# V of token tiles 8 to 15 by a seven-product identity on pairs of tiles, in a fused attention and feed-forward kernel

## The chip, the cores and the metric

The kernel runs on one core of a Trainium2 chip. The metric is the device time of one execution in microseconds (us). The engines of the core work side by side, each through its own queue in order: TensorE (PE: matrix products into the PSUM banks), VectorE (DVE), ScalarE (ACT), GpSimd (POOL, which here only adds and subtracts in SBUF), and SyncE (SP, which issues most of the DMAs).

## The reference

```python
xn = _layernorm(x)                                   # x: 1 x 2048 x 1024, bf16
qkv = xn @ wqkv                                      # wqkv: 1024 x 3072; 32 heads of 32
phi = lambda t: jnp.where(t > 0, t + 1, jnp.exp(t)) + 1e-6
pq, pk = phi(q), phi(k)
kv = einsum("bhsd,bhse->bhde", pk, v);  z = einsum("bhsd->bhd", pk)
o  = (pq @ kv) / (pq @ z + 1e-6)
s  = o @ wo
g  = silu((silu(xn @ w_gate) * (xn @ w_up)) @ w_down)   # 3584 hidden features
return x + s * g
```

The linear attention needs K and V of all 2048 tokens before the first output can be formed. Tokens are cut into 16 tiles of 128.

## The kernel before, in words

The order of the work on PE, DVE, ACT and POOL is written out by hand: each engine takes its instructions in the order in which the program emits them (`manual_schedule`). The work has these stages:

- K and V. For each token tile `i` the loop over `c` runs four products (`emit_Bmm`, L541 to L549): `c` 0 and 1 are the halves of K, 2 and 3 the halves of V. Each is eight matmuls of 128x128 by 128x512 into one of three PSUM banks (`psB`). `emit_Bev` (L551) evacuates a bank: V by an ACT copy, K by `phi`: ACT makes exp (L154) and, up to tile 8, relu (L161) into SBUF; DVE adds a constant (L162) and combines the two (L163). From tile 9 on DVE works in place on the bank (L157, L163). `emit_C(i)` (L564) then adds tile `i`'s K transposed times V to the sum `kvz`, which stays in PSUM.
- In between, DVE prepares the later tiles: `ln_pre` (statistics, L475, L476; the reciprocal root on POOL, L497 and L498) and `emit_N` (normalises, L503; a DMA then transposes the tile into `xnT`).
- `so_stat` (ACT squares rows of W_v and W_o with a sum, L623), `so_pow2` (sums them over partitions on PE and makes a power of two on DVE, L626 to L638), `wo_scale` (DVE scales W_o by it, L641).
- `prep_step` (L352) prepares one tile of the feed-forward weights, in a pipeline of steps: a DMA load on SP, the store of the one before last on SP, an ACT square with a sum (L288), a one-column matmul (L292), three tiny DVE instructions for a power of two (L297 to L301) and a DVE scaling (L311), and four POOL sums (L323 to L326). A weight is squared three steps after its load, scaled and summed in the step after that, and stored one step later still; 22 weights take 26 steps. Four steps lie in tiles 4 to 7, twelve in tiles 8 to 15, two among the Q products of block 0, four each in blocks 1 and 2.
- Q and attention. Tokens go in four blocks of 512. `emit_Q` (L178) makes one of the eight feature tiles of Q, of a block, in five banks (`ps2`); `phi` there takes three ACT instructions and one DVE one (L148 to L151) or the form of K. `emit_ND` (L721) forms the quotient for one token tile: eight small products in one bank group that has no second copy, then DVE (L739, L743, L747). It needs all eight Q feature tiles of its block. Block 0's four run between the Q products of block 1.
- POOL forms sixteen slices of sums of W_o (`To`, L780); the output projection of blocks 2 and 3 uses the seven-product identity with them, and the feed-forward part uses the same identity throughout.

Of the kernel before, what the change touches and what calls it, by code (L numbers as in the profile page):

```python
# [21 lines left out]
def kernel(  # L22
# [37 lines left out]
    NPE = 4  # L60
    NWARM = 11
    NPREP = 13
    NWE = 7
    LEAD = 6
    NPK = 8
    SO_ST = [(i, c) for i in (2, 3, 4, 5) for c in (0, 2)] + [(i, c) for i in (6, 7, 8, 9) for c in (0, 2)]
    PREP_AT = ((4, 1), (5, 1), (6, 1), (7, 1))
    SO_PW = [(7, 1), (10, 1)]
    RXN = 32
# [74 lines left out]

    def emit_phi(work, t_ps, dst, W, in_place=False, act=False):
        e_t = work.tile([P, W], FP32, name="e_t", tag="e_t")
        if act:
            nc.scalar.activation(out=e_t[:], in_=t_ps, func=ACT.Relu, scale=-1.0)  # L148
            nc.scalar.activation(out=e_t[:], in_=e_t[:], func=ACT.Exp, scale=-1.0)
            nc.scalar.activation(out=t_ps, in_=t_ps, func=ACT.Relu)  # L150
            phi_late.append(lambda: nc.vector.scalar_tensor_tensor(out=dst, in0=e_t[:], scalar=EPS, in1=t_ps,  # L151
                                                                   op0=ALU.add, op1=ALU.add))
            return
        nc.scalar.activation(out=e_t[:], in_=t_ps, func=ACT.Exp)  # L154
        if in_place:
            r = t_ps
            nc.vector.tensor_scalar(out=r, in0=t_ps, scalar1=0.0, scalar2=EPS, op0=ALU.max, op1=ALU.add)  # L157
        else:
            r_t = work.tile([P, W], FP32, name="r_t", tag="r_t")
            r = r_t[:]  # L160
            nc.scalar.activation(out=r, in_=t_ps, func=ACT.Relu)  # L161
            nc.vector.tensor_scalar(out=r, in0=r, scalar1=EPS, scalar2=None, op0=ALU.add)  # L162
        nc.vector.scalar_tensor_tensor(out=dst, in0=e_t[:], scalar=1.0, in1=r,  # L163
                                       op0=ALU.min, op1=ALU.add)
# [126 lines left out]
    def emit_st1(key, ps):  # L291
        nc.tensor.matmul(ps, lhsT=ones[:], rhs=st_tiles.pop(key)[:], start=True, stop=True, skip_group_check=True)  # L292
        st_tiles[key] = ps
# [55 lines left out]

    stat_ps = [None]  # L350

    def prep_step(between=None):  # L352
# [36 lines left out]

    kvz_ps = psa_tile("kvz")[1]  # L390
    with ExitStack() as p1:
# [149 lines left out]
        def emit_Bmm(i, c):  # L541
            tok = slice(i * P, (i + 1) * P)
            kv_ps = psB.tile([P, CW], FP32, name="kv_ps", tag="B")
            kv_banks[(i, c)] = kv_ps
            for dc in range(DC):
                mm = nc.tensor.matmul(kv_ps[:], lhsT=xn_ap(dc, tok), rhs=wkv_sb[:, dc, c * CW:(c + 1) * CW],  # L546
                                      start=(dc == 0), stop=(dc == DC - 1))
                if dc == 0 and c == 0:
                    marks[("B", i)] = mm  # L549

        def emit_Bev(i, c):  # L551
            kv_ps = kv_banks.pop((i, c))
            if i not in pkv_tiles:
                pk_sb = work.tile([P, D], BF16, name="pk_sb", tag="pk_sb")
                pkv_tiles[i] = (pk_sb, v_bufs[i % 2])
            pk_sb, v_sb = pkv_tiles[i]
            if c < NCC:
                emit_phi(phiw, kv_ps[:], pk_sb[:, c * CW:(c + 1) * CW], CW, in_place=i >= 9)
            else:
                vc = c - NCC  # L560
                nc.scalar.copy(out=v_sb[:, vc * GPC:(vc + 1) * GPC, 0:P],
                               in_=kv_ps[:].rearrange("p (g c) -> p g c", c=P))

# [13 lines left out]

        warm = work.tile([P, CW], BF16, name="warm", tag="warm")
        nc.vector.memset(warm[:], 0.0)
        wps = psB.tile([P, CW], FP32, name="warm_ps", tag="B")  # L580
        for k in range(NWARM):
            nc.tensor.matmul(wps[:], lhsT=warm[:, 0:P], rhs=warm[:], start=True, stop=True)
        stat_ps[0] = lambda: psC.tile([P, 1], FP32, name="st_ps", tag="C")[:]
# [36 lines left out]
        def so_stat(q):  # L620
            src = wkv_sb[:, q, D:2 * D] if q < 8 else wo_sb[:, q - 8, :]
            with nc.allow_low_precision("a bound that only sets a power of two"):
                nc.scalar.activation(out=pqT_of(0)[:, 2 * (q % 4):2 * (q % 4) + 2, :].rearrange("p a b -> p (a b)"),  # L623
                                     in_=src, func=ACT.Square, accum_out=so_st[:, q:q + 1])

        def so_pow2(h):  # L626
            ps = stat_ps[0]()
            for q in range(8 * h, 8 * h + 8):
                nc.tensor.matmul(ps, lhsT=ones[:], rhs=so_st[:, q:q + 1], start=q == 8 * h, stop=q == 8 * h + 7,
                                 skip_group_check=True)  # L630
# [12 lines left out]

        for i in range(2, NT):
            for c in range(NCH):
                if (i, c) in SO_ST:
                    q = SO_ST.index((i, c))
                    so_stat(q)
                if (i, c) in SO_PW:
                    so_pow2(SO_PW.index((i, c)))  # L650
                if c == 3 and i in WO_SC:
                    wo_scale(WO_SC.index(i))
                if (i, c) != (2, 0):
                    emit_Bmm(i, c)
                if c == 0:
                    emit_C(i - 1)
                emit_Bev(i, c)
                if (i, c) == (2, 2):
                    emit_TR(3)
                if c % 2 == 1:  # L660
                    for k in N_AT.get(2 * i + c // 2, ()):
                        emit_N(k)
                        if 0 <= k - NPE < NCC:
                            load_qo(wo_sb, wo_v, k - NPE)
                    for k in PRE_AT.get(i, ())[c // 2:c // 2 + 1]:
                        ln_pre(k)
                if (i, c) in PREP_AT:
                    prep(1)
                if i >= 8 and c % 2 == 1:
                    k = 2 * (i - 8) + c // 2  # L670
                    prep(12 * (k + 1) // 16 - 12 * k // 16)
        ps1.close()
# [12 lines left out]
        for g in range(1, G):  # L685
            emit_Q(0, g, act=g in (3,5,7))
            if g in (2, 5):
                prep(1)
            phi_flush()
# [24 lines left out]
    with ExitStack() as p2:  # L714
# [10 lines left out]
        def emit_ND(b, t, nd):  # L725
# [12 lines left out]
            for j0, j1, ng in ((0, NJ - 1, GPT), (NJ - 1, NJ, G - (NJ - 1) * GPT)):  # L738
                nc.vector.tensor_scalar(  # L739
                    out=rden[:, j0 * GPT:(j1 - 1) * GPT + ng, :].rearrange("p (j g) h -> p j g h", j=j1 - j0),  # L740
                    in0=nd[:, j0:j1, 0:ng, P:P + HPG], scalar1=EPS,
                    scalar2=rc_all[:, CWO + 1:CWO + 2], op0=ALU.add, op1=ALU.mult)
            nc.vector.reciprocal(out=rden[:, 0:G, :], in_=rden[:, 0:G, :])  # L743
# [116 lines left out]
        def nd_item(b, t):  # L860
            def f():
                raw, nd = psa_tile("nd")

                def nd_ot():
                    emit_ND(b, t, nd)
                    emit_OT(b, t)
                if 0 < b < NB - 1:
                    stat_ps[0] = lambda: raw[:, 0, 511:512]
# [1062 lines left out]
```

## Time and profile before

| what | us |
|---|---|
| median of 3 runs (lowest to highest) | 751.65 (750.5 to 752.22) |
| the profiled execution, its span | 751.34, 749.6 |
| PE busy in the span | 741.9 |
| DVE, ACT, POOL busy in the span | 590.6, 385.6, 403.2 |
| in 25 to 70 (tiles 2 to 7): PE, DVE, ACT, POOL busy of 45 | 45.0, 33.27, 34.77, 6.16 |
| in 85 to 115 (tiles 10 to 13): PE, DVE, ACT, POOL busy of 30 | 30.0, 25.08, 20.80, 29.52 |
| in 145.5 to 159.5 (block 0's quotients, block 1's Q): PE, DVE, ACT, POOL busy of 14 | 14.0, 12.04, 12.43, 13.92 |

PE is busy in nearly every slice of the span. The granted TensorE clock is 1.0 throughout. A busy PE says that a matmul was under way. Other engines may be idle without cost as long as PE never waits for them.

### The profile page before, as it was taken

The numbers are of one execution on the slowest core, as the hardware profiler recorded it, in microseconds if no ns is written. First come the engines' busy times: TensorE is split into PE (matmuls) and PEld (weight loads), VectorE is DVE, ScalarE is ACT, GpSimd is POOL, SyncE is SP. The second block draws the span as 40 slices with busy tenths as digits, with TensorE's granted clock in tenths as the row PEclk, the third lists the DMA queues.
The fourth block names the chain that finished last, engine by engine and source line by source line (L and its number), as shares of the span: only waits on it lengthen the run. The fifth ranks groups of instructions, "written<-read, shape, count | busy, mean of one in ns | idle before, by whom it ended". The sixth has DMA issues, their size and how long they took to land.

```text
span 749.6 us, 11280 instructions
## 1 busy us (share of the span) xinstructions
PE 741.9 (99%) x3962; PEld 370.8 (49%) x3962; DVE 590.6 (79%) x1046; ACT 385.6 (51%) x556; POOL 403.2 (54%) x435
## 2 busy tenths in 40 slices
PE   8999999999999999999999999999999999999997
PEld 3544444454454444444444444644444444467665
DVE  6577788887697688788889886587877767688897
ACT  5677866889965666667557511232222232322023
POOL 0111799998640255858586027310766676770076
PEclk9999999999999999999999999999999999999999
DMA  9957799869678668787889417998698889668854
GB/s 316 337 139 149 219 329 307 310 151 263 208 202 273 229 223 289 274 322 279 320 270 417 169 48 295 269 373 282 225 306 305 307 290 347 244 221 315 279 172 92
DMA packets 132425, 194.21 MB, mean 259 GB/s; under 512 B 36384, under 2 KB 106144, under 8 KB 122640
## 3 DMA queue, kind: packets, MB, share of 16 engines
q1 hardware_dynamic: 123600, 158.69, 65.3%
q0 software_dynamic: 7328, 32.31, 11.6%
q10 hardware_dynamic: 1440, 2.49, 1.0%
q8 instruction: 31, 0.51, 0.3%
q14 instruction: 26, 0.21, 0.1%
HBM read 122.68 MB, written 63.96 MB: 249 GB/s over the span
## 4 chain that ended last, share of the span: by engine, by line
PE 94%; DVE 3%; DMA 1%; ACT 1%; issue 1%; POOL 1%; DVEq 0%; ACTq 0%; POOLq 0%; SPq 0%
PE zw L958 25%; PE kv_ps L546 15%; PE xb L958 13%; PE q_ps L183 6%; PE dzw L1252 6%; PE yb L958 6%; PE dm L1533 5%; PE dm L1497 3%; PE fx L808 3%; PE s_ps L766 3%; PE dx L1252 2%; PE dy L1252 2%; PE dm L1252 1%; PE kvz L568 1%; PE nd L735 1%
## 5 line engine op out<-in xcount | busy, mean ns | idle before, releaser
L958 PEld LDWEIGHTS <-w_sb 128*128 128x128 f16 (+1 forms) x1568 | 152.0, 98 | 183.1 <-issue 0.5
L958 PE MATMUL xb<-xnT,w_sb 128*128 128x512 bf16 x448 | 115.0, 379 | 0.0
L546 PE MATMUL kv_ps<-wkv_sb,xnT 128*128 128x512 bf16 x512 | 113.8, 379 | 0.6 <-ACT xnT L535 0.4
L958 PE MATMUL zw<-xnT,w_sb 128*128 128x512 bf16 x448 | 105.9, 379 | 0.0
L958 PE MATMUL zw<-S,w_sb 128*128 128x512 f16 x448 | 105.8, 379 | 0.0
L323 POOL TENSOR_TENSOR w_sb<-w_sb 128x512 f16<-128x512 bf16 x42 | 50.7, 1206 | 99.9 <-DVE w_sb L311 51.2
L288 ACT ACTIVATE w_sb<-w_sb 128x2048 bf16<-128x2048 bf16 x42 | 79.9, 1902 | 3.5 <-DMA w_sb<-in_B_w_up_dram 2.4
L546 PEld LDWEIGHTS <-xnT 128*128 128x128 bf16 x512 | 48.3, 97 | 56.0 <-ACT xnT L535 0.8
L1139 POOL TENSOR_TENSOR w_sb<-w_sb 128x512 f16<-128x512 f16 (+3 forms) x48 | 50.0, 1063 | 28.5 <-DMA w_sb<-wd 27.5
L1034 ACT ACTIVATE sg<-cg 128x1024 bf16<-128x1024 f32 x28 | 29.6, 1057 | 57.6 <-DVE cg L1027 57.6
L183 PE MATMUL q_ps<-xnT,wq_sb 128*128 128x512 bf16 x256 | 58.4, 379 | 0.4 <-DVE pqT L151 0.4
L958 PE MATMUL yb<-S,w_sb 128*128 128x512 f16 x224 | 57.5, 379 | 0.0
L1027 DVE SCALAR_TENSOR_TENSOR cg<-zw,rc_all,s 128x1024 f32<-128x1024 f32 x28 | 35.9, 1283 | 25.3 <-PE zw L958 12.8
L986 DVE SCALAR_TENSOR_TENSOR s<-yb,rc_all,s 128x512 f32<-128x512 f32 x42 | 31.4, 749 | 27.9 <-ACT s L985 27.9
L324 POOL TENSOR_TENSOR w_sb<-w_sb 128x512 f16<-128x512 bf16 x42 | 50.7, 1207 | 3.3
L1230 POOL DMA_DIRECT2D out_dram<-io x16 | 8.7, 544 | 80.7 <-DVE io L1229 80.5
L326 POOL TENSOR_TENSOR w_sb<-w_sb 128x512 f16<-128x512 bf16 x42 | 50.3, 1197 | 0.0
L325 POOL TENSOR_TENSOR w_sb<-w_sb 128x512 f16<-128x512 bf16 x42 | 49.8, 1185 | 0.0
L985 ACT ACTIVATE s<-xb,rcl 128x512 f32<-128x512 f32 x14 | 9.6, 687 | 65.0 <-PE xb L958 65.0
L985 ACT ACTIVATE s<-xb,rc_all 128x512 f32<-128x512 f32 x42 | 28.4, 675 | 21.9 <-issue 12.7
L311 DVE TENSOR_SCALAR w_sb<-w_sb,cs_all 128x2048 bf16<-128x2048 bf16 x35 | 36.2, 1035 | 3.5 <-DVE cs_all L301 0.8
L183 PEld LDWEIGHTS <-wq_sb 128*128 128x128 bf16 x256 | 24.4, 97 | 28.1 <-issue 0.6
(232 smaller groups left out, 1364.4 us busy)
## 6 DMA issues: line engine op xcount, KB each, us to landing
w_sb<-pk_g SPq DMA_DIRECT2D x27, 1024.0 KB, 6.4
pk_g<-w_sb SPq DMA_DIRECT2D x14, 1024.0 KB, 5.0
w_sb<-pk_u SPq DMA_DIRECT2D x14, 1024.0 KB, 8.5
pk_u<-w_sb POOLq DMA_DIRECT2D x13, 1024.0 KB, 5.5
w_sb<-l SPq DMA_DIRECT2D x12, 896.0 KB, 5.6
l<-w_sb POOLq DMA_DIRECT2D x9, 896.0 KB, 7.7
w_sb<-in_B_w_gate_dram SPq DMA_DIRECT2D x14, 512.0 KB, 6.6
w_sb<-in_B_w_down_dram SPq DMA_DIRECT2D x28, 256.0 KB, 4.7
```

The costliest lines, as they stand in the source:

```text
L183: nc.tensor.matmul(q_ps[:], lhsT=wq_sb[:, dc, g * P:(g + 1) * P], rhs=xn_ap(dc, btok), start=(dc == 0), stop=(dc == DC - 1))
L288: nc.scalar.activation(out=junk, in_=raw_view(key, t), func=ACT.Square, accum_out=asum[:])
L323: nc.gpsimd.tensor_tensor(out=T1, in0=b12, in1=b11, op=ALU.subtract)
L324: nc.gpsimd.tensor_tensor(out=T2, in0=b22, in1=T1, op=ALU.subtract)
L325: nc.gpsimd.tensor_tensor(out=T3, in0=b22, in1=b12, op=ALU.subtract)
L326: nc.gpsimd.tensor_tensor(out=T4, in0=b21, in1=T2, op=ALU.subtract)
L546: mm = nc.tensor.matmul(kv_ps[:], lhsT=xn_ap(dc, tok), rhs=wkv_sb[:, dc, c * CW:(c + 1) * CW], start=(dc == 0), stop=(dc == DC - 1))
L958: mm = nc.tensor.matmul(out, lhsT=lhs(k), rhs=rhs(k), start=(first and k == 0), stop=(k == HK - 1), skip_group_check=True)
L985: nc.scalar.activation(out=s1[:], in_=x_[:], func=ACT.Copy, scale=rc)
L1139: nc.gpsimd.tensor_tensor(out=b(o_), in0=b(a_), in1=b(b_), op=ALU.subtract)
L1252: nc.tensor.matmul(out, lhsT=lhs, rhs=rhs, start=first, stop=lastk, skip_group_check=True)
L1533: nc.tensor.matmul(out, lhsT=lhs, rhs=w[:, j], start=i == 1 and j == 0, stop=j == NQ - 1, skip_group_check=True)
```

## The change

For V of token tiles 8 to 15, two token tiles (rows) and the two halves of the 1024 inputs make a 2x2 block matrix, and W_v is cut in 2x2 blocks likewise. The eight block products of the pair become seven of four matmuls each, with sums of inputs (`S1` to `S4`) and of weights (`T1` to `T4`). The parts:

- `so_pow2(0)` runs at tile 5 and not 7, so the squares of W_v are made earlier (`SO_ST`); DVE then copies the four quarters of W_v, scaled, into the still unused Q feature tiles of blocks 0 and 1 (`wv_copies`, four instructions of 128x2048); POOL forms the four weight sums in place there, each in four slices of 128x512 (`wv_sum`, at (5,0), (5,2), (6,0), (7,2)).
- Tile 7 makes V first, then K; after its V, DVE scales three quarters of W_v in place (`wv_scale`), and after `emit_C(7)` it scales the sum so far (`kv_scale`).
- Each pair makes its products in three banks `X`, `W`, `Y` of `psB`, with the K products in between in the two banks of `psC`. ACT copies X to Y, keeps two partial results in SBUF as float32 over an unused quarter of W_v (`kept_v`), and writes the finished halves; DVE adds the two others (`v_add`).
- `S1` and `S2` are made by DVE, `S3` and `S4` by POOL (`emit_xsum`), before each pair. K is evacuated in place from tile 7 on.
- Preparation steps in tiles 8 to 15 fall from twelve to eight; block 0's Q products take three and not two, and block 0's quotients 1 to 3 one each. The sums of squares there use spare columns of the last `kvz` bank.

The quotient no longer multiplies by W_v's scale (L740). The core of the diff:

```diff
-    SO_PW = [(7, 1), (10, 1)]
+    SO_PW = [(5, 0), (10, 1)]
...
-                emit_phi(phiw, kv_ps[:], pk_sb[:, c * CW:(c + 1) * CW], CW, in_place=i >= 9)
+                emit_phi(phiw, kv_ps[:], pkv_of(i)[0][:, c * CW:(c + 1) * CW], CW, in_place=i >= NV - 1, between=between)
...
+        def wv_copies():
+            for dst, q in ((T1b, (0, 0)), (T3b, (0, 1)), (T2b, (1, 1)), (T4b, (1, 0))):
+                nc.vector.tensor_scalar(out=dst, in0=wv_q(*q), scalar1=c_v, scalar2=None, op0=ALU.mult)
+        def wv_sum(n):
+            T1, T2, T3, T4 = Tv
+            o_, a_, b_ = ((T1, T3b, T1b), (T3, T2b, T3b), (T2, T2b, T1), (T4, T4b, T2))[n]
+            for k in range(HG):
+                nc.gpsimd.tensor_tensor(out=o_[:, k], in0=a_[:, k], in1=b_[:, k], op=ALU.subtract)
+        WV_SUM = ((5, 0), (5, 2), (6, 0), (7, 2))
...
+        def emit_xsum(i):
...
+            nc.vector.tensor_tensor(out=S1, in0=a21, in1=a22, op=ALU.add)
+            nc.vector.tensor_tensor(out=S2, in0=S1, in1=a11, op=ALU.subtract)
+            nc.gpsimd.tensor_tensor(out=S3, in0=a11, in1=a21, op=ALU.subtract)
+            nc.gpsimd.tensor_tensor(out=S4, in0=a12, in1=S2, op=ALU.subtract)
...
+            if i >= NV and n == 1:
+                prep(1)
+        for i in range(2, NV):
+            for n, c in enumerate(range(NCH) if i < NV - 1 else (2, 3, 0, 1)):
+                before(i, n)
                 if (i, c) != (2, 0):
                     emit_Bmm(i, c)
+                if (i, n) == (NV - 1, 2):
+                    wv_scale()
+                if n == 0:
                     emit_C(i - 1)
                 emit_Bev(i, c)
...
+                behind(i, n)
+                if (i, n) == (NV - 2, 3):
+                    emit_xsum(NV)
...
+        for i in range(NV, NT, 2):
+            j = i + 1
...
+            mm4(X, xn_q(i, 0), wv_q(0, 0), True)
+            nc.scalar.copy(out=Y[:], in_=X[:])
+            mm4(W, S1, Tv[0], True)
+            emit_Bmm(i, 0)
+            if i == NV:
+                emit_C(i - 1)
+            emit_Bev(i, 0)
...
+            mm4(Y, S2, Tv[1], False)
+            mm4(X, xn_q(i, 1), wv_q(1, 0), False)
+            if i == NV:
+                kv_scale()
+            nc.scalar.copy(out=kept_v(0), in_=by_half(W[:]))
+            nc.scalar.copy(out=v_half(i, 0), in_=by_group(X))
+            nc.scalar.copy(out=kept_v(1), in_=by_half(Y[:]))
+            behind(i, 1)
+            before(i, 2)
+            emit_Bmm(i, 1)
+            if i > NV:
+                emit_C(i - 1)
+            mm4(Y, S3, Tv[2], False)
+            emit_Bev(i, 1, between=lambda: v_add(j, Y, 0))
...
+            emit_Bmm(j, 0)
+            emit_Bev(j, 0)
...
+            mm4(Y, xn_q(j, 1), Tv[3], False)
+            mm4(W, S4, wv_q(1, 1), False)
+            nc.scalar.copy(out=v_half(j, 0), in_=by_group(Y))
+            v_add(i, W, 1)
+            if j + 1 < NT:
+                emit_xsum(j + 1)
+            behind(j, 1)
+            before(j, 2)
+            emit_Bmm(j, 1)
+            emit_C(i)
+            emit_Bev(j, 1)
...
-            if g in (2, 5):
+            if g in (2, 4, 6):
                 prep(1)
...
-                if 0 < b < NB - 1:
+                if b < NB - 1 and (b, t) != (0, 0):
                     stat_ps[0] = lambda: raw[:, 0, 511:512]
                     prep_step(nd_ot)
```

## The prediction

> **What bounds the kernel now.** I read the page first, for the share of each engine; then the chain that ended last, for the places where PE itself waits; then the order of time on DVE, ACT and POOL around the change. The page (columns: slices of the span; groups by line):
>
> ```profile
> span 749.6 us, 11280 instructions
> PE 741.9 (99%) x3962; PEld 370.8 (49%) x3962; DVE 590.6 (79%) x1046; ACT 385.6 (51%) x556; POOL 403.2 (54%) x435
> ...
> L546 PE MATMUL kv_ps<-wkv_sb,xnT 128*128 128x512 bf16 x512 | 113.8, 379 | 0.6 <-ACT xnT L535 0.4
> ```
>
> PE sets the time; V and K cost 113.8 us and wait 0.6. In the chain (start, length, what), products follow each other from tile 2 to the end of block 0 without a gap. The first break is in block 1, where a DVE scaling of a weight takes 4.23 us:
>
> ```profile
> 40.64 6.91 PE kv_ps L546 x32
> 47.55 0.46 PE kvz L568 x8
> ...
> 145.37 0.47 PE nd L735 x8
> ...
> 164.43 4.23 DVE w_sb L311
> ```
>
> So 32 matmuls take 6.91 us, 0.216 each, and work removed from PE is worth its full time only while no other engine is late. How near they are shows in the order of time (start, length, engine, line). DVE and POOL around 97 us:
>
> ```profile
> 96.73 1.15 POOL L325 TENSOR_TENSOR w_sb<-w_sb 128x512 f16<-128x512 bf16 x1
> 97.84 1.60 POOL L326 TENSOR_TENSOR w_sb<-w_sb 128x512 f16<-128x512 bf16 x1
> ...
> 97.09 1.34 DVE L311 TENSOR_SCALAR w_sb<-w_sb,cs_all 128x2048 bf16<-128x2048 bf16 x1
> 98.35 1.64 DVE L641 TENSOR_SCALAR wo_sb<-wo_sb,cs_all 128x2048 bf16<-128x2048 bf16 x1
> ```
>
> A scaling from SBUF to SBUF (0.74 at its shortest) and a POOL sum (1.15) do not overlap: each waits for the other and they take turns. Then around block 0's quotients:
>
> ```profile
> 144.29 0.69 DVE L151 SCALAR_TENSOR_TENSOR pqT<-e_t,q_ps 128x512 bf16<-128x512 f32 x1 [0.22 <-ACT q_ps L150]
> ...
> 145.00 0.66 PEld L735 LDWEIGHTS <-pqT 128*128 128x128 bf16 x8
> ...
> 163.61 4.50 POOL L780 TENSOR_TENSOR To_sb<-wo_sb,To_sb 128x512 f16<-128x512 bf16 x4
> ...
> 164.43 4.23 DVE L311 TENSOR_SCALAR w_sb<-w_sb,cs_all 128x2048 bf16<-128x2048 bf16 x1
> ```
>
> The first quotient's weights load 0.02 us after DVE finishes the last Q feature tile: no slack there. And against four sums of the `To` form in a row, the scaling got no turn until the row was over.
>
> The sum goes against the profiled execution's own 751.34 us (span 749.6, 1.7 around it), 0.3 under the median 751.65 of three runs. No change means within 0.2%, 1.5 us.
>
> **A. Products.** Each pair does 28 matmuls for V where it did 32: 16 fewer, at 0.216, is -3.45. Float16 ones show the same 379 ns as bf16 ones (L958), so nothing is lost on the type.
>
> **B. Tiles 5 to 8.** DVE is 33.27 busy of 45 us in tiles 2 to 7, and gets there: a power of two (0.75, as at 64.63 to 65.3), four copies (0.75 each, L311's shortest), `S1` and `S2` (0.42 to 0.66 in L801 to L804, 1.0 together), three scalings of W_v (2.25), and tile 7 in place (0.70 and 0.69 for each half, 2.9 against 2.4). PE's own clock: tile 5 starts at 45.82, plus 0.18 for the eight small matmuls; with 1.73 a product and 0.46 a `kvz` step it wants `C(5)` at 55.1, `X` at 68.1, and `W` at 69.0. `W` takes the bank of K(7,0), so it needs DVE through that evacuation. DVE is free at 48.05 (end of the L476 at 47.80). Until then it must do: 0.75 + 3.0 + tile 5's K 2.4 + two normalisations and two statistics 4.0 + tile 6's K 2.4 + the same 4.0 + sums 1.0 + one normalisation and statistics 2.0 + scalings 2.25 + K(7,0) 1.45 = 23.25, hence 71.3. That is 2.3 late even if POOL never interferes: the low end.
>
> POOL now puts sixteen slices of 1.11 us in the same stretch, where it had 1 us a tile. Queued on POOL behind them are the roots (L497, L498) for tiles 10 to 15, which the normalisations need; I find those in time. For scalings and normalisations I take turns, as at 97 us. For K's last step from SBUF (L163, two float32 inputs) no row lies next to POOL work: beside it, with one input in PSUM, it keeps 0.69; the two-input L1228 goes from 0.42 to 0.91. I let L163 pass freely and `S1`, `S2` wait. Then `T1`'s slices start at 50.4; the fourth copy ends at 52.8, K(5) at 56.1 (PE waits 1.0); `T3`'s and `T2`'s slices push tile 6's work to 67.8, the sums to 70.2, the first scaling to 73.5 (`X` wanted at 69.1: 4.3), K(7,0) to 77.0 (`W` wanted at 74.4: 2.6). B = 7.9. If L163 waits too, the same walk gives 2.7 + 1.7 + 4.1 + 3.0 = 11.5: the high end with turns. The cover for pricing the earlier squares (ACT) and the six XnT transposes on SP at nothing is idle time: ACT 34.77 of 45, SP waits on nothing new here; if it went, 1.25 a square.
>
> **C. The pairs.** PE alone needs 60 matmuls and two `kvz` steps, 13.9 a pair. DVE: 5.8 for K, 1.4 for two adds (0.69, L1255), 1.0 sums, 3.3 for two preparations, plus normalisations and `kv_scale` (about 1.4 each) in the first, `wo_scale` (2.6) in the next two: 14.3, 14.7, 14.1, 10.6. ACT is in order: behind `X`'s second product come two copies (0.5 each), the preparation's square (1.9), in the first pair a square of W_o (1.25), and only then K's exp; DVE's first step and `v_add` (0.7 each) follow, and `Y`'s last product waits on that add. From the end of `X` that is 0.5 + 0.5 + 1.9 + 0.6 + 1.4 = 4.95 with gaps 5.05, against 1.73 + 0.46 + 0.86 + 1.73 = 4.8 on PE: 0.25 late; in the first pair (no `kvz` step there) 6.3 against 4.3: 2.0. In pairs 10 and 12 `wo_scale` goes ahead of the second add, and `C(i)` is 0.75 late. C = 2.0 + 3 x 0.25 + 2 x 0.75 = 4.2; between 0 (ACT's square slips behind) and 6 (the POOL turns again). Four preparations fewer free 7.6 of ACT and 18 of POOL there, but PE did not wait on those before.
>
> **D. Block 0.** A preparation moved here brings all its instructions: load and store on SP, square 1.9 on ACT, one small matmul, 0.55 + 0.75 or more on DVE, 4.6 on POOL. The Q products of block 0 get one more: ACT ends the last feature tile 18.3 after the first Q product starts, not 16.7, and the first quotient, with no slack (above), goes 1.3 late. Block 0's quotients get three. ACT works 1.77 on each Q tile of block 1, two make 3.54 where PE takes 3.93, and two squares of 1.9 now lie ahead of the last: its feature tile is ready at 37.2, and block 1's first quotient wanted it at 34.8: 2.4 late. Sum 3.7; low end 2. Queue order: the added preparations' POOL sums fall behind the sixteen `To` slices (18 us), and SP's store of each waits for them with the next load and the quotient's transpose behind it; by the same walk the loads are late by up to 3.4 us in block 1, where eight S and Q items are run ahead, so I price it at 0 with 3.4 as the upper bound.
>
> Sum: 751.34 - 3.45 + 7.9 + 4.2 + 3.7 = 763.7. The rest of the change (quotient's constant, spare columns for small sums) is free: no instruction more.
>
> **Rivals.**
> *The lateness is swallowed.* PE's run-ahead over three K and five Q banks takes up DVE's and ACT's lag, as it did in 10 to 159 us at 84% busy DVE. Place: `W`'s bank. It decides if DVE reaches K(7,0)'s end by 69.0, in 21 us for my 23.25, and ACT likewise saves its 2 us in block 0. Then only A and about 1 remain: 749. Against it: the counted rows, and the 0.02 us.
> *DVE never waits for POOL* (POOL yields always): B 2.3, C 2.5, D 3.7: 756.4. The alternating rows speak against it.
> *All two-input steps wait too:* B 11.5: 767.3. L1228's rows speak for it. By the Trainium skill ("SBUF — State Buffer", Who interferes with whom) a VectorE instruction with two SBUF inputs contends with a GpSimd one that reads SBUF, and whichever comes second is blocked until the first finishes, which is this rival; the turns at 97 us agree with its blocking, the 4.23 us, over three further ends of a sum, do not.
> *DVE gets no turn in a row of slices.* The 4.23 us against L780 is the only row in which a scaling meets this very form, and `wv_sum` and block 0's three scalings would meet it. In tiles 5 to 8, rows of four and eight slices hold DVE until K(7,0) ends near 83: B 14. In block 0, a scaling asked for at 26.8 after its first Q product waits for the end of `To` near 41; the next quotient waits with it: 14 more. 751.34 - 3.45 + 14 + 4.2 + 17.7 = 784. For T sums of the same shape at 183 us DVE did get its turn (0.82).
>
> **How the numbers follow.** Chances: swallowed 0.18; DVE never waits 0.22; my walk 0.25; two-input steps wait 0.15; no turns 0.20, half of it under 780 where only one of the two places shows it. The forecast is 763.7, itself between 759 and 768. Range 748.5 to 780: below lies 0.06, above 0.12. Faster 0.18; same, from the low edge of the second case, 0.04; slower 0.78.
>
> **What would show it.** Right: PE idle before `C(5)`, before the first pair's `X` and `W` (released by DVE) and before block 1's first quotient; DVE copies, L162 and L503 longer than 0.75, 0.43 and 0.52 while `wv_sum` runs. Wrong: no PE idle time from 50 to 80; a first quotient of block 1 that follows its Q product at once; or a scaling in block 0 of 4 us and more (the last rival).

## The result and the profile after

The changed kernel takes 786.5 us (median of four runs, 785.4 to 787.9), the kernel before 751.4 in the same session: 1.0468 times as long, with a 95% interval of 1.0446 to 1.049. The forecast was 763.7, its range ended at 780. The sign was right, the size was not: 35 us were lost where 12 were expected, and they were lost in other places.

The profiled execution took 787.9 (span 786.1), 1.4 above its median, and is set against the 751.3 (span 749.6) of before. First the page, its span and engines.

```profile
span 786.1 us, 11254 instructions
PE 743.1 (95%) x3883; PEld 370.5 (47%) x3946; DVE 607.5 (77%) x1071; ACT 385.0 (49%) x556; POOL 433.4 (55%) x459
```

PE is as busy as before (743.1 against 741.9) although 16 products are gone, and it stands for 43 us where it stood for 8. (This trace has 3883 product records for 3946 weight loads: 63 products are under way but not recorded.) So nothing was bought, and the question is where PE stands. The waits of PE by what ended them (total, times, longest) answer it:

```profile
PE nd L295 <- DVE tot L301: 9.5, 1, 9.5
PE nd L295 <- ACT w_sb L291: 4.3, 4, 1.8
PE vx L757 <- DVE wkv_sb L682: 3.8, 1, 3.8
PE kvz L582 <- DVE tot L301: 3.2, 3, 1.7
PE kvz L582 <- DVE pk_sb L166: 3.1, 2, 1.6
PE vw L757 <- DVE pk_sb L166: 2.3, 1, 2.3
PE kvz L295 <- DVE kvz L686: 1.5, 1, 1.5
...
PE kv_ps L554 <- ACT wkv_sb L791: 1.0, 2, 0.5
PE kv_ps L554 <- DMA wkv_sb<-in_A_wqkv_dram: 0.7, 1, 0.7
```

The lines with `vx`, `vw` and `pk_sb` are the first pair and tiles 5 and 6 (9.2 us together, forecast as B). The lines where `kvz` waits for `tot` or for L686, and K's product for L791, lie in the pairs (6.0). The `nd` lines lie in the blocks, and the first of them, 9.5 us in one piece, was not in the forecast at all. The last line is a wait near 9 us, at the start of this one execution.

Three points of the trace divide the span into stages: the end of the last `kvz` product, the first product of block 0's quotients (`nd`), and the first product into `xb` in the feed-forward part. Their times, and the stages between them, for most of the runs (us):

| run | last `kvz` product ends | from the first `nd` to the first `xb` product | median time |
|---|---|---|---|
| before | 129.8 | 99.9 | 751.4 |
| after | 146.5 | 118.1 | 786.5 |
| before, preparations moved | 129.5 | 118.5 | 769.1 |
| the same, S store on SP | 129.8 | 107.4 | 759.5 |
| the same as the third, `To` spread | 129.4 | 113.0 | 763.7 |
| before, S store on SP alone | 129.7 | 99.7 | 751.1 |
| before, `To` spread alone | 129.4 | 106.1 | 757.8 |
| after, `To` spread | 145.7 | 109.8 | 777.6 |
| after, S store on SP | 146.4 | 107.5 | 776.2 |
| after, no W_v sums | 136.1 | 119.8 | 778.8 |
| after, preparation one stage later | 142.2 | 119.2 | 783.2 |
| after, in place from tile 5 | 143.2 | 118.1 | 782.8 |
| after, 28 idle products added | 143.9 | 116.5 | 781.8 |

Between the first two points lie 15.4 us in both kernels. Of the 36.5 us between the two profiled executions, 16.8 arise up to the last `kvz` product and 18.2 in the blocks; the last 1.5 arise in the feed-forward part of this one execution (506.0 us, against 504.1 to 505.7 in the other profiles) and belong to no step. Nor do 0.9 of the 16.8: in this execution alone a product waits 0.65 us for the load of its weights near 9 us, and the first `kvz` step starts at 25.1 us, where it starts between 23.9 and 24.4 in all other runs. That leaves 15.9.

Up to the last `kvz` product the 15.9 divide as follows. The removed products give -3.45 (16 at 0.216). The gaps of tiles 5 to 8 give 9.2, those of the pairs 6.0. Behind the gaps of `X` and `W` products run at half pace, 2.1 more. And each stop costs 0.16 beyond its gap, since the last product ahead of it isn't overlapped by a next one (0.379 to its end against 0.216 to the next start): the 11 stops in these gaps are 1.8. The sum is 15.65; some 0.2 stay open.

Here is PE from tile 5 to the first pair, in order of time (start, length, engine, line, what; in brackets the idle time ahead and what ended it):

```profile
57.91 0.40 PE L582 MATMUL kvz<-v_sb,pk_sb 128*128 128x129 bf16 x4 [1.62 <-DVE pk_sb L166]
...
66.92 0.40 PE L582 MATMUL kvz<-v_sb,pk_sb 128*128 128x129 bf16 x4 [1.46 <-DVE pk_sb L166]
...
76.26 1.55 PE L757 MATMUL vx<-wkv_sb,xnT 128*128 128x512 bf16 x4 [3.76 <-DVE wkv_sb L682]
80.16 1.89 PE L757 MATMUL vw<-pqT,xs 128*128 128x512 f16 x4 [2.34 <-DVE pk_sb L166]
...
84.82 1.02 PE L757 MATMUL vy<-pqT,xs 128*128 128x512 f16 x4
```

`C(5)`, `X` and `W` wait for DVE where the forecast had put them (1.0, 4.3 and 2.6 there), and `C(6)` waits too. The four products of `W` take 1.89 us, the four of `Y`, of the same kind, 1.02. DVE in the same stretch:

```profile
54.30 1.52 DVE L166 SCALAR_TENSOR_TENSOR pk_sb<-e_t,r_t 128x512 bf16<-128x512 f32 x1
...
57.16 0.69 DVE L166 SCALAR_TENSOR_TENSOR pk_sb<-e_t,r_t 128x512 bf16<-128x512 f32 x1
...
78.08 0.69 DVE L166 SCALAR_TENSOR_TENSOR pk_sb<-e_t,kv_ps 128x512 bf16<-128x512 f32 x1
```

K's last step with both inputs in SBUF (L166, `e_t` and `r_t`) takes 1.52 while a row of four W_v slices runs on POOL (50.83 to 56.84), and 0.69 just behind that row. With one input in PSUM (`kv_ps`, tile 7) it takes 0.69 beside three slices too (POOL has them from 77.31 to 80.67). So steps with two SBUF inputs wait for GpSimd as well, which was one of the rivals.

Now the blocks. POOL, SP and ACT around the long stand of block 1, one fence for each (on the queues of SP and ACT the lines are DMA issues):

```profile
183.09 4.49 POOL L930 TENSOR_TENSOR To_sb<-wo_sb,To_sb 128x512 f16<-128x512 bf16 x4
...
191.44 1.16 POOL L330 TENSOR_TENSOR w_sb<-w_sb 128x512 f16<-128x512 bf16 x1
```

```profile
192.63 0.33 SPq L345 DMA_DIRECT2D pk_g<-w_sb  x1
...
197.63 0.33 SPq L345 DMA_DIRECT2D pk_g<-w_sb  x1
```

```profile
192.47 0.66 ACT L919 ACTIVATE s_sb<-s_ps,s_sc 128x512 bf16<-128x512 f32 x1
203.94 0.34 ACTq L922 DMA_DIRECT2D s_dram<-s_sb  x1
204.38 0.60 ACT L149 ACTIVATE e_t<-q_ps 128x512 f32<-128x512 f32 x1 [11.25 <-DMA pk_g<-w_sb]
```

A preparation's sums (L327 to L330) stand on POOL behind the sixteen sums of `To`, which end at 187.6. SP's store of that preparation (L345) is issued at 192.63, and SP has issued nothing since 174.4 (the end of its issues of L228). The next store leaves at 197.63. ACT has finished an S tile at 193.1 and is to issue the store of it (L922); in the trace it is released only when SP's second store has landed (at 203.86), although the two have no data in common. Both stores raise the same semaphore in the trace's records (number 107), and the later one in the program waits on it before it is issued. Behind the store in ACT's order stand the exponentials of Q, and so PE stands for 9.5 us.

### The profile page after: what moved, and what is told of

Read it like the earlier page. It is cut to its first block, busy times and chain, and to the rows that moved or that the text cites. A ratio compares the mean times of both kernels' runs of the same rounds, so it can differ in the third digit from the quotient of the medians.

```text
span 786.1 us, 11254 instructions
## 1 busy us (share of the span) xinstructions
PE 743.1 (95%) x3883; PEld 370.5 (47%) x3946; DVE 607.5 (77%) x1071; ACT 385.0 (49%) x556; POOL 433.4 (55%) x459
## 5 line engine op out<-in xcount | busy, mean ns | idle before, releaser
L1108 PE MATMUL xb<-xnT,w_sb 128*128 128x512 bf16 x421 | 113.2, 379 | 2.5 <-ACT sg L1183 1.0
L327 POOL TENSOR_TENSOR w_sb<-w_sb 128x512 f16<-128x512 bf16 x42 | 49.8, 1185 | 113.6 <-DVE w_sb L315 50.9
L1108 PE MATMUL zw<-xnT,w_sb 128*128 128x512 bf16 (+1 forms) x447 | 105.8, 379 | 0.1
L554 PE MATMUL kv_ps<-wkv_sb,xnT 128*128 128x512 bf16 x373 | 88.1, 381 | 2.8 <-ACT wkv_sb L791 1.0
L554 PEld LDWEIGHTS <-xnT 128*128 128x128 bf16 x384 | 36.6, 98 | 48.3 <-issue 7.0
L1177 DVE SCALAR_TENSOR_TENSOR cg<-zw,rc_all,s 128x1024 f32<-128x1024 f32 x28 | 35.9, 1283 | 24.4 <-PE zw L1108 13.3
L328 POOL TENSOR_TENSOR w_sb<-w_sb 128x512 f16<-128x512 bf16 x42 | 49.5, 1177 | 3.3
L330 POOL TENSOR_TENSOR w_sb<-w_sb 128x512 f16<-128x512 bf16 x42 | 50.5, 1202 | 0.0
L329 POOL TENSOR_TENSOR w_sb<-w_sb 128x512 f16<-128x512 bf16 x42 | 49.4, 1175 | 0.0
L152 DVE SCALAR_TENSOR_TENSOR pqT<-e_t,q_ps 128x512 bf16<-128x512 f32 x27 | 18.2, 682 | 31.4 <-ACT q_ps L151 31.3
L186 PEld LDWEIGHTS <-wq_sb 128*128 128x128 bf16 x256 | 24.4, 98 | 27.6 <-issue 0.5
```

Of the source, the lines that this page charges most:

```text
L186: nc.tensor.matmul(q_ps[:], lhsT=wq_sb[:, dc, g * P:(g + 1) * P], rhs=xn_ap(dc, btok), start=(dc == 0), stop=(dc == DC - 1))
L327: nc.gpsimd.tensor_tensor(out=T1, in0=b12, in1=b11, op=ALU.subtract)
L328: nc.gpsimd.tensor_tensor(out=T2, in0=b22, in1=T1, op=ALU.subtract)
L329: nc.gpsimd.tensor_tensor(out=T3, in0=b22, in1=b12, op=ALU.subtract)
L330: nc.gpsimd.tensor_tensor(out=T4, in0=b21, in1=T2, op=ALU.subtract)
L1108: mm = nc.tensor.matmul(out, lhsT=lhs(k), rhs=rhs(k), start=(first and k == 0), stop=(k == HK - 1), skip_group_check=True)
```

## The experiments

The reading above makes two claims about the blocks: the `To` sums make SP late, and ACT's store carries that lateness to PE. The rival is that ACT and the loads are simply overloaded, or late from the pairs. For tiles 5 to 8 the claims are turns between DVE and POOL on top of 2.3 us of DVE's own work; for the pairs, the place of the small sums; for the slow products, the stand ahead of them.

**The S store on SP's queue.**

```
-                nc.scalar.dma_start(out=s_dram[r0:r0 + P, :], ...
+                nc.sync.dma_start(out=s_dram[r0:r0 + P, :], ...
```

> The changed kernel with the store of each finished S tile issued from SP's queue in place of ACT's (9 stores). Theory (the ACT queue stands because its store shares a completion count with the late prepared-weight store): ACT no longer stands 11.25 us, and the 9.47 us gap and the slow products behind it go: 773 to 777. Rival (PE's gap comes from the late loads, transposes or scalings themselves, and ACT's wait only lay beside it): 782 to 787.

Measured: 776.2 (ratio to before 1.0328, 1.0312 to 1.0343), 10.3 less than the changed kernel. PE's 9.47 us gap is gone, and no gap of the blocks is longer than 1.3 now. The waits of SP in this run:

```profile
SPq L345 <- POOL w_sb L330: 59.3, 11, 18.3
```

SP is still 18.3 us late, as it was in the changed kernel (18.1). What is gone is the way by which the lateness reached PE. What is left of it is seen on ACT, which stands 3.45 us in block 1 for a weight load that SP issued late, and on PE right behind it, 0.67.

**`To` spread.** The four groups of `To` sums go behind the four quotients of block 1.

```
-        for o_, a_, b_ in ((To[0], bb[0][1], bb[0][0]), ...):   # ahead of block 0
-            for k in range(HG):
-                nc.gpsimd.tensor_tensor(out=o_[:, k], ...)
...
                 else:
                     nd_ot()
+                if b == 1:
+                    to_group()          # four sums of To
```

> The changed kernel with GpSimd's sixteen To sums taken out of block 0 and put in four groups of four, one behind each quotient of block 1. Theory (queue order): block 0's preparations no longer find 18 us of To sums ahead of their own sums, SP's stores and the loads and transposes behind them go on time, and the 11.25 us stand of ACT and the 9.47 us gap of PE in block 1 go, with the half-speed products behind them: 772 to 776. Rival (ACT simply has too much to do in block 0 and 1 with three squares more): the gap stays, 784 to 788.

Measured: 777.6 (1.0346, 1.033 to 1.0362). The gap of 9.47 and the stand on ACT are gone, 8.9 us in all, less than expected: three new gaps (1.8, 0.7 and 2.2) stand at 243 to 250 us, ahead of block 3's quotients and a product of the output identity.

**The moved preparations without any change to V.** This is the kernel before, with one preparation a tile in tiles 8 to 15, three beside block 0's Q products and three at its quotients.

```
-                if i >= 8 and c % 2 == 1:
-                    k = 2 * (i - 8) + c // 2
-                    prep(12 * (k + 1) // 16 - 12 * k // 16)
+                if i >= 8 and c == 1:
+                    prep(1)
...
-            if g in (2, 5):
+            if g in (2, 4, 6):
...
-                if 0 < b < NB - 1:
+                if b < NB - 1 and (b, t) != (0, 0):
```

> The kernel before with the changed placement of the preparations alone (one a tile in tiles 8 to 15, three beside block 0's Q products, three at its quotients 1 to 3; To where it was; no product removed). Theory (queue order): the same stand in block 1 comes without any change to V: 9.5 to 14 for it and about 2 in block 0, 762 to 768. Rival (the stand is inherited from the lateness of the pairs): 751 to 755.

Measured: 769.1 (1.0234, 1.0218 to 1.0249), 17.4 slower than before and just above the range expected. Its waits, PE first, then ACT, then SP:

```profile
PE nd L292 <- ACT e_t L148: 8.5, 1, 8.5
...
ACT e_t L148 <- DMA pk_g<-w_sb: 10.5, 1, 10.5
...
SPq L341 <- POOL w_sb L326: 65.2, 13, 18.2
```

In the kernel before the last of these lines reads 45.5, 13, 4.6. The stage of the blocks is as long as in the changed kernel (118.5 and 118.1), so half of the loss has nothing to do with the identity on V.

**Two by two.** The same kernel with each of the two edits, and each edit alone on the kernel before.

> The kernel before, the preparations placed as in the changed kernel, and the S tiles' store on SP's queue. Theory (ACT's store is what turns SP's lateness into a stand): 769.1 less the 8.5 us gap and the slow products behind it, 758 to 760; left are the waits of block 0, 4 to 5, and some of the late loads. Rival (late loads and transposes stop TensorE by themselves): 764 or more.

> The kernel before, the preparations placed as in the changed kernel, and the sixteen To sums in groups of four behind block 1's quotients. Theory (the To sums ahead of the preparations' sums make SP late in the first place): the gap goes, 757 to 761, unless the groups hold VectorE at block 3's quotients as in the changed kernel. Rival (SP is late by the three added preparations alone): 766 to 769.

> The kernel before with the S tiles' store on SP's queue and nothing else. Theory (with its own placement SP's stores are late by 4.6 us at most, and ACT never stands on them): no change, 750.5 to 752.5. Rival (the move helps by itself): under 750.

> The kernel before with the To sums in groups of four behind block 1's quotients and nothing else. Theory: no sum waits behind To in block 0 there, so nothing is gained but the 4.23 us scaling's turn (hidden): 750.5 to 753. Rival (the groups hold up VectorE at block 3's quotients): 754 or more.

Measured: 759.5 (1.0108, 1.0093 to 1.0123) with the store moved, 763.7 (1.0165, 1.015 to 1.018) with `To` spread; as controls 751.1 (0.9993, 0.9984 to 1.0002) and 757.8 (1.0091, 1.0074 to 1.0108). The store alone changes nothing where SP is not late, and takes 9.6 off where it is. Spreading `To` costs 6.2 by itself (here the rival was right) and takes 5.3 off, so it undoes about 11.5 of the moved preparations' cost. The 763.7 fell between what the theory and its rival had expected, since it has both the gain and the 6.2. Either edit removes the stand: it takes both, sums ahead on POOL and a store on ACT that waits. With the store moved, the same 18.2 us of SP's lateness are left with little effect:

```profile
SPq L341 <- POOL w_sb L326: 59.3, 11, 18.2
```

What is left of the cost in that kernel, 7.9 us, is mostly block 0: gaps of 0.49, 1.50, 1.10 and 1.35 before quotients and the small products ahead of them (behind ACT's squares), 1.11 at an S product of block 1, 0.16 for each stop, and seven products at half pace behind the gap of 1.35 (1.5 together).

In the control with `To` spread, PE has gaps of 1.9, 0.6 and 2.3 at 223 to 229 us and some seven products at half pace behind them, which make up the 6.2. A part of their cause is seen on DVE. The four sums L804 to L807, with two SBUF inputs, take 0.42 each when nothing runs on POOL (L801 to L804 of the kernel before, at 221 us):

```profile
215.83 1.16 DVE L804 TENSOR_TENSOR wq_sb<-oT 128x512 f16<-128x512 bf16 x1
...
218.20 1.37 DVE L806 TENSOR_TENSOR wq_sb<-oT 128x512 f16<-128x512 bf16 x1
```

In this run POOL is still at the sums of block 2's preparations, up to 223 us, and DVE takes turns with them; the `To` groups stand ahead of them. The four sums take 5.05 in place of 1.7. Ahead of the last of the three gaps DVE also stands 2.57 us for a DMA into `oT`; why that one is late stays open.

**W_v's sums left out.**

```
-            if (i, n) in WV_SUM:
-                wv_sum(WV_SUM.index((i, n)))
```

> The changed kernel without GpSimd's sixteen slices of sums of W_v (so V of tiles 8 to 15 is made from wrong sums); copies, scalings and everything else stay. Theory (turns with the slices put 6.9 of the 9.2 us of idle PE in tiles 5 to 8 on top of 2.3 from DVE's own work): idle before C(5) and C(6) gone, 2 to 3 us left at the first pair, 778 to 780. Rival (VectorE's own added work is what is late): 784 to 787. Second rival (VectorE alone is not late at all): 775 to 777.

This kernel leaves out the sums, so its V of tiles 8 to 15 is wrong; only its time counts here.

Measured: 778.8 (1.037, 1.035 to 1.0391). The last `kvz` product ends 10.4 earlier, of which 0.9 is the late start of the changed kernel's profile. Of the gaps of tiles 5 to 8 only `W`'s is left:

```profile
PE vw L755 <- DVE pk_sb L166: 2.7, 1, 2.7
```

The forecast had worked out 2.3 for DVE's own added work by counting rows; 2.7 is what it is. All else of the gaps in this stretch goes with the slices.

**In place from tile 5**, so that K's last step reads PSUM.

```
-... in_place=i >= NV - 1, ...
+... in_place=i >= 5, ...
```

> The changed kernel with K's feature steps of tiles 5 and 6 also done in place in PSUM, so that VectorE's last step has one input in SBUF and one in PSUM. Theory (steps with two SBUF inputs wait for GpSimd's slices, 1.52 in place of 0.69, and the in-place form does not): the four gaps of tiles 5 to 8 shrink by 2.5 to 4 us: 782.5 to 784. Rival (only VectorE's total work counts, and the in-place first step is longer, 0.70 for 0.43): 786 to 788.

Measured: 782.8 (1.0418, 1.04 to 1.0435), 3.8 less. The gaps are now 1.8 ahead of a product of tile 5, 0.9 at `X` and 3.8 at `W`: 6.4 for 9.2. The edit takes DVE's steps L165 and L166 out of the turns, and ACT's relu of these tiles goes with them; the two together are worth that much, and the run does not part them.

**The preparation one stage later in the pairs.**

```
-            if i >= NV and n == 1:
+            if i >= NV and n == 2:
```

> The changed kernel with the preparation of each tile of a pair taken one stage later (behind the tile's third stage, not its second). Theory (the small sum has its column in the bank of the kvz sums, so the next kvz step waits until VectorE has read that column, and in the first pair the small matmul waits for the scaling of that bank): the waits of 1.74, 0.86, 0.63 and 0.35 and the 1.48, with 0.16 for each stop, go: 780 to 782. Rival (VectorE or ScalarE is late with K and V themselves, as the forecast had it): 785 to 788.

Measured: 783.2 (1.0426, 1.041 to 1.0441), 3.3 less, where 4.5 to 6.5 were expected; the last `kvz` product ends 4.2 and 3.5 earlier than in the runs with the store on SP and with `To` spread, whose code is the changed kernel's up to there. The waits of a `kvz` step for `tot` and the wait for L686 are gone. Two others are left in the pairs:

```profile
PE kv_ps L554 <- ACT wkv_sb L791: 2.1, 4, 0.5
```

K's product waits for ACT's copy of a kept product, because that copy goes into a quarter of `wkv_sb`, the tile which the product reads. The other (0.8) is the second power of two, whose eight small products stand behind such a column's reading. The gap of block 1 is 10.8 here for 9.5, which takes back part of the gain.

**Idle products ahead of `X` and `W`.** The 28 products go into a spare bank that nothing reads.

```
+            fill(16)
             mm4(X, xn_q(i, 0), wv_q(0, 0), True)
             nc.scalar.copy(out=Y[:], in_=X[:])
+            fill(12)
             mm4(W, S1, Tv[0], True)
```

> The changed kernel with 28 idle products (K columns of W_v's neighbour into a spare bank, never read) on TensorE: 16 ahead of the first pair's X, 12 ahead of its W, where it stands still for 3.8 and 2.3 us. Theory (products run at half pace for some 1 to 3 us after TensorE has stood): the twelve slow products behind the two gaps go, 2.3 us: 784 to 785 although 28 products were added. Rival (the slow pace has another reason, such as the float16 operands or the late sums): no gain or the added products show, 786 to 788.

Measured: 781.8 (1.0404, 1.0388 to 1.0419): 28 products more, 4.7 us less. PE in this run:

```profile
71.32 3.62 PE L780 MATMUL fill_ps<-wkv_sb,xnT 128*128 128x512 bf16 x16
75.16 1.04 PE L757 MATMUL vx<-wkv_sb,xnT 128*128 128x512 bf16 x4 [0.23 <-DVE wkv_sb L682]
76.04 2.75 PE L780 MATMUL fill_ps<-wkv_sb,xnT 128*128 128x512 bf16 x12
79.15 1.04 PE L757 MATMUL vw<-pqT,xs 128*128 128x512 f16 x4 [0.36 <-DVE pk_sb L166]
```

`X` and `W` run at 0.216 a product now, where they ran at up to 0.43, with the same operands. From the start of `C(5)` to the end of the last `kvz` product this run takes 89.1 us; the changed kernel and the runs with the store on SP and with `To` spread, whose code is otherwise the same up to there, take 90.7, 91.5 and 90.6. So 1.5 to 2.4 are gained there, for the 2.3 expected. Another 1.6 lie in the blocks, where the changed kernel's gap of 1.8 at 231 us is missing in this run. The cause of that, and the remaining 0.7 to 1.6, stay open.

**Three edits together** (store on SP, preparation later, in place from tile 5).

> Store on SP's queue, preparation one stage later and in place from tile 5, all three together. If the three causes are separate, their gains add: 776.2 less 5.5 less 3: 767 to 769. If one only covered another: 771 or more.

Measured: 768.4 (1.0229, 1.0214 to 1.0245). The single gains, 10.3, 3.3 and 3.8, add up to a time of 769.1: three separate causes.

**The identity on pairs 10 to 15 only**, with W_v's sums a tile apart.

```
-    NV = 8
+    NV = 10
...
-    PREP_AT = ((4, 1), (5, 1), (6, 1), (7, 1))
+    PREP_AT = ((4, 1), (5, 1), (6, 1), (7, 1), (8, 0), (8, 2), (9, 0), (9, 2))
...
-        WV_SUM = ((5, 0), (5, 2), (6, 0), (7, 2))
+        WV_SUM = ((5, 1), (6, 1), (7, 1), (8, 1))
...
-                if b < NB - 1 and (b, t) != (0, 0):
+                if 0 < b < NB - 1 or (b, t) == (0, 3):
```

> As the run with three edits, but in place from tile 9, with the identity on tile pairs 10 to 15 only (three pairs), W_v's sums one group a tile in tiles 5 to 8, four preparations in tiles 8 and 9 and only one at block 0's quotients. Theory (the 9.2 us and slow products of tiles 5 to 8 come from too little time between W_v's power of two and the first pair): that stretch loses nearly all of its 12 us, 0.9 is given back by one pair fewer, and block 0 gains 2 to 3: 753 to 757. Rival (the turns on VectorE cost the same wherever they lie): 762 or more.

Measured: 769.9 (1.025, 1.0234 to 1.0265). The gaps are 1.6, 1.5, 1.5, 4.8 and 5.6, 14.9 in all, so more time did not help, and the time is where the rival had put it. Whether the turns cost the same wherever the slices lie is not shown: tiles 8 and 9 bring four preparations' sums to POOL besides, and K's steps are in place only from tile 9. The other half of the expectation held: with one preparation at block 0's quotients and the store on SP, the blocks take 100.2 us, against 99.9 before.

**Tile 7 in another order, then W_v scaled by ACT, then fewer preparations in block 0.** Each run adds to the one above it, starting from the three edits.

```
-... else (2, 3, 0, 1)):
+... else (0, 2, 3, 1)):        # and C(6) last, W ahead of X in the first pair
```

> The run with three edits, and tile 7 in the order K(7,0), V(7,0), V(7,1), K(7,1) with C(6) last and W ahead of X in the first pair, so that W and X take banks which ScalarE frees. Theory (VectorE is late by a fixed amount and PE only has to wait because W's bank is K(7,0)'s): the gaps of 3.77 and 0.87 and the slow products go down, 762 to 765. Rival (the lateness shows at the next place, C(7) or the scaled W_v): 767 to 769.

```
-                nc.vector.tensor_scalar(out=dst, in0=wv_q(*q), scalar1=c_v, ...)
+                nc.scalar.activation(out=dst, in_=wv_q(*q), func=ACT.Copy, scale=c_v)
...
-                nc.vector.tensor_scalar(out=wv_q(*q), in0=wv_q(*q), scalar1=c_v, ...)
+                nc.scalar.activation(out=wv_q(*q), in_=wv_q(*q), func=ACT.Copy, scale=c_v)
```

> The same with the four scaled copies and three scalings of W_v on ScalarE, which is half idle in tiles 5 to 7, in place of VectorE. Theory (VectorE's own 5.25 us and their turns with GpSimd are what is left in tiles 5 to 7): another 1.5 to 3 less than the order alone: 760 to 763. Rival (ScalarE becomes late with K's exponentials and the scaling stands between V(7,1) and X): no less than the order alone.

```
-            return wkv_sb[:, 2 * k:2 * k + 2, D + CW:2 * D].bitcast(FP32)
+            # a tile of the pool of normalised x, idle by then
...
-            if i >= NV and n == 2:
+            if i >= NV and (n == 2 or (i, n) in ((11, 0), (15, 0))):
...
-                if b < NB - 1 and (b, t) != (0, 0):
+                if 0 < b < NB - 1 or (b, t) == (0, 3):
```

> The same, with the kept products in a spare tile (not in W_v's quarter), the second power of two one stage later, two more preparations in the pairs and only one at block 0's quotients. Theory: the four waits of 0.51 and the 0.81 go (3.6 with 0.16 for each stop), block 0 loses 2 to 2.5: 754 to 757. Rival (preparations in the pairs cost there what they cost in block 0): 759 or more.

Measured: 764.5 (1.0176, 1.0161 to 1.0191), 767.2 (1.0215, 1.0198 to 1.0232) and 761.7 (1.0135, 1.012 to 1.015). The order alone is worth 3.9: `W` no longer waits for K(7,0), and `X`'s gap is 1.6. ACT's scaling loses 2.7 again: a gap of 2.6 appears ahead of `C(7)`, and ACT's squares come 2.8 late in block 1; the rival was right. The last step takes 5.5 off: the blocks take 100.4 us for 107.7, while the last `kvz` product ends 2.3 later, with two more preparations in the pairs and new waits, such as this one (and 2.1 at a small sum; the 2.6 ahead of `C(7)` stays):

```profile
PE kvz L582 <- DVE v_sb L773: 2.8, 2, 1.6
```

So preparations in the pairs do cost, less than in block 0. No version with the identity came below the kernel before; this one, 1.35% above it, is the best.

## Why the prediction was wrong

**The step that failed is the last sentence of D.** It named the right queue: the added preparations' sums fall behind the sixteen `To` sums, and SP's store waits with everything behind it. It then put the lateness of the loads at up to 3.4 us and priced it all at 0. Two things were wrong. SP stood 18.1 us at a single store, until the rest of the `To` row (13.1) and that preparation's own sums (5.0) were over, and all that SP issues stood behind it. And the walk followed SP's loads and transposes only. It did not ask what ACT's own queue issues in block 1: its store of each S tile, which the trace shows released by SP's late store. That SP's lateness by itself is nearly harmless was a right guess (18.2 us late at 759.5 us), and so was its bound of 3.4 for the loads (ACT stands 3.45 for one in the changed kernel with the store on SP); neither was any help. The two-by-two shows the cost: 9.6 us through ACT's store, 10.3 in the changed kernel.

**The rest of D** was right in kind: the squares on ACT bring block 0's quotients late. The forecast was 3.7, of which 1.3 at the first quotient and 2.4 at the first of block 1. The run with moved preparations and the store on SP shows 0.49 and, up to block 1's first quotient, 1.50, 1.10 and 1.35, with further stops and slow products 7.9 in all. The 1.3 does not come out of the prediction's own 18.3 and 16.7 (1.6), and its 4.95 in C adds up to 4.9; neither matters beside the rest. D as a whole is 18.2 by the stages, for 3.7.

**B** was 7.9; its four gaps are 9.2. Three of the four places and what ends the waits were right, and the 2.3 for DVE's own work was measured at 2.7. Two terms were mis-sized. The step "I let L163 pass freely" is refuted by the 1.52, and the in-place run (3.8 us) agrees: the rival with two SBUF inputs was right here, as its walk had `C(6)` late too (1.7; measured 1.46). It is the rule of the Trainium skill ("SBUF — State Buffer", Who interferes with whom) that a VectorE instruction with two SBUF inputs contends with a GpSimd one that reads SBUF; the trace agrees, 1.52 against 0.69. And the sum had no term for what comes behind a stand: 2.1 at half pace, and 0.16 for each stop.

**C** was 4.2 and its gaps are 6.0, but that is not a near hit. The waits it names (K's exponential behind ACT's square, then the add, then `Y`'s last product) don't occur. What occurs is in the sentence that ends the sum: that the spare columns for small sums are free, since they add no instruction. They add a wait: the column lies in the bank of the `kvz` sums, and the next `kvz` step stands until DVE has read it. The run with the preparation one stage later removed these waits.

**A** (16 products at 0.216) was not tried by itself; nothing in the traces contradicts it.

**The rivals.** "The lateness is swallowed" and "DVE never waits for POOL" fall with the 9.2 us. "DVE gets no turn" gave 784, near the time, and is refuted as a mechanism by its own sign: a scaling in block 0 of 4 us and more. Block 0's scalings beside the `To` rows, in the changed kernel:

```profile
170.46 0.75 DVE L315 TENSOR_SCALAR w_sb<-w_sb,cs_all 128x2048 bf16<-128x2048 bf16 x1
...
186.39 1.74 DVE L315 TENSOR_SCALAR w_sb<-w_sb,cs_all 128x2048 bf16<-128x2048 bf16 x1
```

The two between them took 1.45 and 1.14. Here DVE gets its turn after one slice at most. The row of 4.23 us in the kernel before, from which that rival was built, comes again at the same place in the run with the S store on SP alone (4.23 at 164.4 us), so it is no accident of one execution; it stays unexplained.

In sum: -3.45, 7.9, 4.2 and 3.7 were forecast, and the stages show -3.45, then 19.35 for B and C with their slow products and stops, then 18.2 for D. The signs that the prediction had named for being right all came (PE idle ahead of `C(5)`, `X`, `W` and block 1's first quotient, 0.55 there; 1.37 for 0.43 on DVE beside the slices). They could not show that a term was missing.

## What to carry to other kernels

When work is moved to another stage, walk the queues of every engine that issues a DMA there, and ask of each issue what it may be held by; a store that is late for its own reason can stop an engine that has no data in common with it, and an otherwise swallowed lateness of 18 us becomes 10 us of the span. A wait needs no new instruction: a spare column in a bank, or a spare quarter of a tile, joins whoever uses the rest of it. And to an engine that sets the time every stop costs more than its gap, so price the stops too.

## What the runs showed of the hardware

- After PE had stood for 3.8 us and for 9.5 us, products of 512 columns started 0.427 us apart, about ten of them at `X` and `W` and eight behind the long stand; behind its stands of 1.3 to 1.8 us they started 0.216 apart. But short stands close together can bring it too, in some executions: in the run with the S store on SP, seven products started 0.427 apart behind stands of 1.1, 1.3 and 0.5 us between 176 and 183 us (granted clock 0.86 from 175 to 187), where the changed kernel has the same stands and keeps its pace. In the windows of the changed kernel (start and end, length, busy time and instructions of PE, PEld, DVE, ACT and POOL, the granted clock, DMA):

```profile
70.00:76.00 6.00, 2.50 (x12) 0.94 (x10) 5.90 (x11) 4.62 (x8) 5.40 (x7) 1.00 0.81 178
76.00:80.00 4.00, 1.55 (x4) 0.37 (x4) 3.93 (x7) 0.57 (x1) 3.92 (x5) 0.58 0.68 164
80.00:90.00 10.00, 8.31 (x37) 3.69 (x39) 5.34 (x11) 4.33 (x7) 2.02 (x3) 0.83 0.15 30
```

  The granted clock falls to 0.58 and 0.83 there and is 1.00 in all three windows once idle products fill the gaps. By the Trainium skill ("TensorE: Matmul & The Clock Gate", What's actually happening) the clock is halved after an idle window of some 3.4 us; the stands of 3.8 and 9.5 us agree with it. The slow products behind the three short stands, none of them near 3.4 us, are not covered by it.
- Beside a row of GpSimd sums, DVE's steps take turns one by one: 1.37 for 0.43 (one float32 input) and 1.52 for 0.69 (two) in the changed kernel, 1.16 to 1.37 for 0.42 (two 16-bit inputs) in the control with `To` spread. With one of two inputs in PSUM the step keeps its 0.69. One scaling of the kernel before was held to the end of such a row (4.23 us, in two kernels alike).
- ACT stood 11.25 us because a DMA issue on its queue waited for the landing of a store that SP had issued, with the same semaphore and no data in common. Moving it to SP's queue took 10.3 us off this kernel and nothing off the kernel before.
